# Last sequence of an FFT convolution with spectral mixing: its transformed signal stored by halves of 64 positions, its result tiles in two groups of six

## The chip, the cores and the metric

One core of one Trainium2 chip. The metric is the device time of one execution in microseconds, taken as the median of several runs. Five engines work side by side: TensorE (PE, with its weight loads shown apart as PEld), VectorE (DVE), ScalarE (ACT), GpSimd (POOL) and SyncE (SP), which here issues transfers. Sixteen DMA engines move data between HBM and the on-chip memory (SBUF). TensorE writes its results to PSUM, eight banks of 512 fp32 values on each of 128 partitions.

## The reference

x is 8 sequences of S = 5696 positions with 128 channels, h a filter of the same length. With `n` = 2S:

```
a = irfft(rfft(x, 2S) * rfft(h, 2S))[:, :S]        # long convolution
A = rfft(a);  Y = 0
Y[:, :64] = A[:, :64] mixed by 64 complex 128x128 matrices (w_r, w_i)
u = a + irfft(Y, n=S)
out = u + max(u @ w_ch, 0)                         # float32, 8 x 5696 x 128
```

## The kernel before, in words

A position is written as `J*q + p`, with J = 64, p in 0..63 and q in 0..88 (NQ = 89). The kernel goes over four pairs of sequences (`g_` = 0..3, `b` = 0, 1 within a pair). A first long phase (to about 268 us) makes the spectra, multiplies them by the filter's and leaves them in HBM. The change concerns the second phase, which makes u and the output.

**u tiles.** The 64 values of p are cut into four blocks of 16 (`c_`, NCH = 4), each into two halves of 8. `u_tile` (L787) makes one half: two wide matmuls against `IBs` and 16 narrow ones against `S4a` and `S4b` give 8 p x 89 q in two PSUM banks, and one copy (`evac`, L800) writes those 712 columns as fp16 to the sequence's `UT` buffer. Before, that buffer lies in the natural order of positions: element `J*q + p`. The copies go to ACT or DVE by a fixed pattern of eight (L798: five on ACT, three on DVE).

**Result tiles.** `o_tile` (L841) takes u back as matmul weights: four matmuls of 256 columns (L864) against `WI` (w_ch beside the identity) give u @ w_ch and u, transposed to positions on partitions, in two banks. ACT makes R = relu (L870), DVE adds u (L871) into an output buffer, SP sends the buffer out (L882). With NW = S // 128 = 44, tile r4 takes positions `44*partition + 4*r4 + j`: eleven full tiles (128 partitions x 4 positions), and a twelfth of the last 64 positions with one matmul ("small tile" below). Two neighbouring tiles share one output buffer and one transfer ("wide", 4 KB from each partition). In the last sequence before the change, r4 0 to 7 are wide, 8 to 10 go out singly (2 KB from each partition), and then the small one.

**Order.** All instructions are recorded in program order for each engine; what depends on what is worked out by the recorder. Both kinds of tile take PSUM in turn from four slots of two banks (`LSLOT`), so that the fifth tile waits for the first one's reader. `o_tile` uses seven wide output buffers (`O`), four single ones (`Os`) and three `R` buffers in turn. The order of tiles is the loop at L887 to L903: result tiles stand in a list `todo`, and after each u half some are taken from it. In the last pair (`last`, L894) the order is the four blocks of sequence b = 0 and then the four of b = 1; block number n = 0..7, half 0 and 1:

```
for _ in range((2, 2 + half)[n >= NCH] if last else 1 + half):
```

So two tiles follow each half in n = 0 to 3, and two or three in n = 4 to 7. Each result tile needs all of its sequence's u (L861 names all eight halves). At the last pair's start 24 tiles of the pair before are in `todo`; 12 of b = 0 join after n = 3, and 12 of b = 1 after the loop. I number the last pair's 48 tiles 0 to 47 in the order in which they are taken, and write (n,half) for a u half. Before the change 16 are taken in n = 0 to 3, 20 in n = 4 to 7, and the last twelve (36 to 47) follow when all u is made: the tail. Tiles 11, 23, 35 and 47 are small.

Of the kernel before, what the change touches and what calls it, by code (L numbers as in the profile page):

```python
# [4 lines left out]
P = 128  # L5
# [118 lines left out]
def bass_long_conv_fft__then__afno_spectral_mix_kernel(nc, x, h, moe_w_r, moe_w_i, moe_w_ch, out):  # L124
    B, S, D = x.shape
    M = moe_w_r.shape[0]
    assert D == P and M == 64 and B == 8
    J = 64
    NQ = S // J
# [3 lines left out]
    NP = B // 2  # L133
# [26 lines left out]
    rows = s4.transpose(1, 0, 2, 3).reshape(2 * NK, S)  # L160
# [45 lines left out]
    def at(name, cols, dt, off):  # L206
        return nc.alloc_sbuf_tensor_at(name, [P, cols], dt, offset=off)
# [48 lines left out]
    ZB = 16  # L256
# [13 lines left out]
    u_sb = [at(f"UT{i}", S, F16, u_off[i]) for i in range(4)]  # L270
# [21 lines left out]
    def pv(bank, off, dims, p0=0, n=P):  # L292
        return bass.AP(ps, p0 * 4096 + bank * 512 + off, [[4096, n]] + [list(d) for d in dims])
# [5 lines left out]
    def bank(i):  # L299
        return ("bank", i)  # L300
# [3 lines left out]
    def evac(dst, src, reads, writes, scale=None, eng=None, after=()):  # L304
        e = eng
        if e is None:
            turn[0] ^= 1
            e = "scalar" if turn[0] else "vector"
        if e == "scalar":
            if scale is None:  # L310
                R.add(e, lambda h_: h_.copy(dst, src), reads, writes, after=after)  # L311
            else:
                R.add(e, lambda h_: h_.activation(dst, src, COPY, scale=scale), reads, writes, after=after)  # L313
        elif scale is None:
            R.add(e, lambda h_: h_.tensor_copy(dst, src), reads, writes, after=after)  # L315
        else:
            R.add(e, lambda h_: h_.tensor_scalar_mul(dst, src, scale), reads, writes, after=after)  # L317

    def dma(eng, dst, src, ring, reads=(), writes=(), after=()):
        R.add(eng, lambda h_: h_.dma_start(dst, src), reads, writes, ring=ring, after=after)  # L320

    def mm(o, l, r, st, sp, reads, writes):
        R.add("tensor", lambda h_: h_.matmul(o, l, r, start=st, stop=sp), reads, writes)  # L323
# [3 lines left out]
    def once(key, toks):  # L327
        if key in first:
            return []
        first[key] = 1  # L330
        return list(toks)
# [3 lines left out]
    def turns(name, items):  # L335
        i = ring2.get(name, 0)
        ring2[name] = i + 1
        return items[i % len(items)]
# [101 lines left out]
    for j in range(16):  # L440
        t = turns("h", [0, 2, 4])
# [5 lines left out]
        for i in range(4 if j < 15 else 26):  # L447
# [4 lines left out]
             eng="vector" if j in (3, 7) else "scalar")  # L452
# [264 lines left out]
    for j in range(32):  # L717
        a_tile(j, FOUR)
        if j >= 11 and j % 3 == 2 and (j - 11) // 3 < LH:
            h_ = turns("s", FOUR)  # L720
            filter_tick((j - 11) // 3, [h_, h_ + 1])
    keep(16, turns("s", FOUR))
    for g_ in range(NP):
# [15 lines left out]
        if g_ + 1 < NP:  # L739
            for j in range(6, 32):  # L740
# [3 lines left out]
                if wp and j % 2 == 1:  # L744
                    dst, src_, ring, tok = wp.pop(0)
# [7 lines left out]
        clear_zt(i)  # L753

    LSLOT = [0, 2, 4, 6]
    NCH = J // ZB
    n_ev = [0]
    ahead = {}

    def u_z(i, b, half, alone=False, parts=(0, 1)):  # L760
        g_, c_ = divmod(i, NCH)
        t = ahead.get((i, b, half))
        if t is None:
            t = turns("l", LSLOT)
        z = zt[i % NC]
        for hb in parts:
            if not alone:
                u_c(i, b, half, t, hb, True)
            for pl in range(4):
                for ri in range(2):  # L770
                    pz = half * 8 + hb * 4 + pl
                    so = (c_ * ZB + pz) * NQ
                    n = (P, PB + RB)[ri]
                    mm(pv(t + hb, pl * NQ, [[1, NQ]]), z[ri][0:n, pz * 256 + b * P:pz * 256 + b * P + P], s4_sb[ri][0:n, so:so + NQ],
                       alone and pl == 0 and ri == 0, not alone and pl == 3 and ri == 1, [("zt", i % NC, ri), ("zt0", i % NC), ("s4", ri, 0)] + ([("s4", ri, 1)] if c_ >= NCH // 2 else []), [bank(t + hb)])
        if alone:
            ahead[(i, b, half)] = t
        return t

    def u_c(i, b, half, t, hb, first_):  # L780
        g_, c_ = divmod(i, NCH)
        pl0 = half * 8 + hb * 4
        mm(pv(t + hb, 0, [[1, 4 * NQ]]), c_sb[:, (2 * g_ + b) * P:(2 * g_ + b + 1) * P],
           ib_sb[:, (c_ * ZB + pl0) * NQ:(c_ * ZB + pl0 + 4) * NQ], first_, not first_,
           [("c", g_ // 2), ("ib", 0)] + ([("ib", 1)] if c_ >= NCH // 2 else []), [bank(t + hb)])

    def u_tile(i, b, half):  # L787
        g_, c_ = divmod(i, NCH)
        t = ahead.get((i, b, half))
        if t is None:  # L790
            t = u_z(i, b, half)
        else:
            for hb in range(2):
                u_c(i, b, half, t, hb, False)
        ub = (g_ % 2) * 2 + b
        old = {0: WT, 1: WT, 2: U_ALL, 3: U_ALL}[ub]
        n_ev[0] += 1
        e = "scalar" if n_ev[0] % 8 in (0, 2, 3, 5, 7) else "vector"  # L798
        src = pv(t, 0, [[1, NQ], [512, 2], [NQ, 4]])
        evac(bass.AP(u_sb[ub], c_ * ZB + half * 8, [[S, P], [J, NQ], [4, 2], [1, 4]]),  # L800
             src, [bank(t), bank(t + 1)], [("u_", ub, 2 * c_ + half)], eng=e, after=once(("u", ub), old))

    XTT = [(n, g_) for g_ in range(NP) for n in ("xt", "xtn")]
    reflect("vector", s4_sb[0], P, 0, ("s4", 0), M_ALL[1:4])
# [13 lines left out]
    for hb in range(2):  # L818
        evac(bass.AP(y_sb, hb * 32 * B, [[2 * M * B, P], [B, 32], [M * B, 2], [1, B]]),
             pv(6 + hb, 0, [[2 * B, 32], [B, 2], [1, B]]), [bank(6 + hb)], [("y", hb)], eng="vector" if hb else "scalar",  # L820
             after=ZY)
# [16 lines left out]
    NW = S // P  # L838
    TAIL = S - NW * P

    def o_tile(g_, b, r4):  # L841
        ub = (g_ % 2) * 2 + b
        bb = 2 * g_ + b
        t = turns("l", LSLOT)
        i = n_o[0]
        n_o[0] += 1
        full = r4 < NW // 4
        last_ = (g_, b) == (NP - 1, 1)
        wide = r4 < (8 if last_ else NW // 4 // 2 * 2)
        big = wide or (last_ and full)  # L850
        h_ = r4 % 2 if wide else 0
        if big:
            if not h_:
                o_cur[0] = turns("o8", list(range(NO8)))
            ob, key, old = o8_sb[o_cur[0]], ("o8", o_cur[0]), o8_old[o_cur[0]]
        else:
            k_ = turns("os", list(range(NO)))
            ob, key, old = o_sb[k_], ("os", k_), o_old[k_]
        OW = 1024 if big else 512
        n, rows = (4, P) if full else (1, TAIL)  # L860
        rd = [("u_", ub, c_) for c_ in range(2 * NCH)] + [("wch",), ("i16",)]  # L861
        for j in range(n):
            lh = bass.AP(u_sb[ub], 4 * r4 + j, [[S, P], [NW, P]]) if full else u_sb[ub][:, NW * P:S]
            mm(pv(t + j // 2, (j % 2) * 256, [[1, 256]], 0, rows), lh, WI, True, True, rd, [bank(t + j // 2)])  # L864
        bk = [bank(t), bank(t + 1)] if full else [bank(t)]
        rs = r_sb[i % NR]
        rv = bass.AP(rs, 0, [[512, rows], [P, n], [1, P]])
        ov = bass.AP(ob, h_ * 512, [[OW, rows], [P, n], [1, P]])
        src_r, src_u = pv(t, 0, [[256, n], [1, P]], 0, rows), pv(t, P, [[256, n], [1, P]], 0, rows)
        R.add("scalar", lambda e: e.activation(rv, src_r, RELU), bk, [("r", i % NR)], after=once(("r", i % NR), G_ALL + XTT + [("y", 0), ("y", 1), ("id",)]))  # L870
        R.add("vector", lambda e: e.tensor_tensor(ov, src_u, rv, ADD), bk + [("r", i % NR)],  # L871
              [key + (h_,)], after=once(key, old))
        if wide and not h_:
            return
        w_ = (2 if wide else 1) * 4 * D
        if full:
            dst = bass.AP(out.tensor, out.offset + bb * S * D + (4 * r4 - 4 * h_) * D, [[NW * D, P], [1, w_]])
            src = ob[:, 0:w_]
        else:
            dst = bass.AP(out.tensor, out.offset + bb * S * D + NW * P * D, [[D, TAIL], [1, D]])  # L880
            src = ob[0:TAIL, 0:P]
        dma("sync", dst, src, "o", [key + (v_,) for v_ in range(h_ + 1)])  # L882

    todo = []
    NB = NCH * NP
    NW4 = NW // 4 + 1
    for g_ in range(NP):  # L887
        last = g_ == NP - 1
        order = [(c_, b) for b in range(2) for c_ in range(NCH)] if last else [(c_, b) for c_ in range(NCH) for b in range(2)]
        for n, (c_, b) in enumerate(order):  # L890
            i = NCH * g_ + c_
            for half in range(2):
                u_tile(i, b, half)
                for _ in range((2, 2 + half)[n >= NCH] if last else 1 + half):  # L894
                    if todo:
                        o_tile(*todo.pop(0))
            if b == 1 and i + NC < NB:
                load_zt(i + NC)
            if last and n == NCH - 1:
                todo += [(g_, 0, r4) for r4 in range(NW4)]  # L900
        todo += [(g_, b, r4) for b in range(1 if last else 0, 2) for r4 in range(NW4)]
    while todo:
        o_tile(*todo.pop(0))  # L903
    R.add("sync", lambda e: e.nop(), [], [("o8", i, v_) for i in range(NO8) for v_ in range(2)] + [("os", i, 0) for i in range(NO)])
# [31 lines left out]
```

## Time and profile before

| | |
|---|---|
| median of 3 runs (lowest, highest) | 385.36 us (385.15, 385.92) |
| the profiled execution: its own time | 385.31 us |
| its span in the profile | 383.2 us |
| busy share of the span: PE, DVE, ACT, POOL | 94%, 79%, 81%, 22% |
| mean granted clock of TensorE | 0.992 |
| output transfers on SP (O and Os) | 57 |

The span runs from the first to the last instruction that the profile shows; the execution's own time is 2.1 us longer. Times in the text are counted from the span's start. "Busy" of PE counts matmuls that overlap, so the start of the next tile's first matmul says more than the busy share. Transfers are issued by SP and land later; the profile gives for each group the median time from issue to landing.

### The profile page before, as it was taken

The numbers are of one execution on the slowest core, as the hardware profiler recorded it, in microseconds if no ns is written. First come the engines' busy times: TensorE is split into PE (matmuls) and PEld (weight loads), VectorE is DVE, ScalarE is ACT, GpSimd is POOL, SyncE is SP. The second block draws the span as 40 slices with busy tenths as digits, with TensorE's granted clock in tenths as the row PEclk, the third lists the DMA queues.
The fourth block names the chain that finished last, engine by engine and source line by source line (L and its number), as shares of the span: only waits on it lengthen the run. The fifth ranks groups of instructions, "written<-read, shape, count | busy, mean of one in ns | idle before, by whom it ended". The sixth has DMA issues, their size and how long they took to land.

```text
span 383.2 us, 12465 instructions
## 1 busy us (share of the span) xinstructions
PE 360.0 (94%) x5346; PEld 277.7 (72%) x5346; DVE 303.1 (79%) x346; ACT 310.7 (81%) x489; POOL 84.4 (22%) x134
## 2 busy tenths in 40 slices
PE   7789899999989999989999899999999999999992
PEld 7778766667856667856657766668898988898871
DVE  3549899988998998989998988766347766777784
ACT  8469689998989997899997899994566776777783
POOL 8703011100733210832212312427000000000000
PEclk9999999999999999999999999998999999999998
DMA  7999959988999995999995899999999999999776
GB/s 140 208 286 362 251 141 240 241 230 240 94 126 202 259 262 167 123 123 246 247 256 129 113 329 347 331 382 399 381 394 359 402 407 417 403 403 361 290 281 275
DMA packets 87201, 103.94 MB, mean 271 GB/s; under 512 B 22883, under 2 KB 72675, under 8 KB 83591
## 3 DMA queue, kind: packets, MB, share of 16 engines
q1 hardware_dynamic: 62667, 67.76, 50.9%
q0 software_dynamic: 24480, 35.40, 43.8%
q8 instruction: 42, 0.69, 0.7%
q14 instruction: 12, 0.10, 0.1%
HBM read 70.61 MB, written 51.12 MB: 318 GB/s over the span
## 4 chain that ended last, share of the span: by engine, by line
PE 73%; DVE 7%; DMA 6%; ACT 6%; issue 3%; POOL 3%; DVEq 0%; POOLq 0%
PE ps L323 73%; DMA Xr<-in_x_dram 4%; DVE As L317 2%; DMA Xt<-in_x_dram 2%; DVE U L630 2%; POOL Xr L320 2%; ACT As L313 2%; ACT R L870 1%; ACT Zs L311 1%; ACT UT L311 1%; POOL Hin L320 1%; DVE Xin L365 1%; DVE Hs L315 1%; ACT Zt L311 1%; ACT Xs L311 1%
## 5 line engine op out<-in xcount | busy, mean ns | idle before, releaser
L638 DVE TENSOR_TENSOR U<-Xs,Hs 128x2048 f16<-128x2048 f16 (+1 forms) x73 | 86.9, 1193 | 13.4 <-ACT Xs L311 12.5
L323 PE MATMUL ps<-U,Wc 128*128 128x512 f16 (+1 forms) x368 | 94.1, 376 | 0.5 <-DVE U L630 0.5
L311 ACT CAST Xs<-ps 128x1024 f16<-128x1024 f32 (+1 forms) x77 | 75.2, 980 | 11.9 <-PE ps L323 6.9
L311 ACT CAST Zs<-ps 128x512 f16<-128x512 f32 (+1 forms) x132 | 69.3, 597 | 1.8 <-PE ps L323 1.8
L871 DVE TENSOR_TENSOR O<-ps,R 128x512 f32<-128x512 f32 x81 | 52.5, 686 | 19.8 <-ACT R L870 12.5
L870 ACT ACTIVATE R<-ps 128x512 f32<-128x512 f32 x96 | 50.9, 573 | 14.3 <-PE ps L323 13.9
L317 DVE TENSOR_SCALAR As<-ps 128x720 f16<-128x720 f32 x70 | 57.7, 886 | 5.2 <-PE ps L323 4.6
L323 PE MATMUL ps<-F,Xin 128*128 128x180 f16 x512 | 53.7, 249 | 3.8 <-DVE Xin L365 2.5
L323 PE MATMUL ps<-As,M 64*128 64x128 f16 x1440 | 50.3, 217 | 3.5 <-DVE U L630 2.9
L323 PEld LDWEIGHTS ps<-F,Xin 128*128 128x128 f16 x512 | 44.4, 155 | 12.6 <-DVE As L317 2.8
L323 PE MATMUL ps<-WI,UT 128*128 128x256 f16 x360 | 51.8, 278 | 0.5 <-DVE O L871 0.4
L313 ACT ACTIVATE As<-ps 128x720 f16<-128x720 f32 (+1 forms) x61 | 45.7, 769 | 7.9 <-PE ps L323 6.4
L323 PEld LDWEIGHTS ps<-U,Wc 128*128 128x128 f16 x368 | 28.6, 97 | 29.4 <-ACT Zs L311 3.7
L323 PEld LDWEIGHTS ps<-As,M 64*128 64x128 f16 x1440 | 40.6, 94 | 9.7 <-DVE U L630 3.6
L311 ACT CAST UT<-ps 128x712 f16<-128x712 f32 x40 | 30.0, 752 | 18.0 <-PE ps L323 17.0
L323 PEld LDWEIGHTS ps<-WI,UT 128*128 128x128 f16 x360 | 39.3, 152 | 4.2 <-issue 1.9
L323 PE MATMUL ps<-IBs,C 128*128 128x356 f16 x128 | 39.9, 321 | 0.6
L320 POOL DMA_DIRECT2D Xt<-in_x_dram x40 | 21.4, 540 | 80.3 <-PE ps L323 79.8
L323 PEld LDWEIGHTS ps<-G,Zs 128*128 128x128 f16 x512 | 26.1, 96 | 14.5 <-ACT Zs L311 2.0
L638 DVE TENSOR_TENSOR U<-ps,Hs 128x2048 f16<-128x2048 f32 x15 | 34.3, 2285 | 0.0
L323 PE MATMUL ps<-G,Zs 128*128 128x128 f16 (+2 forms) x512 | 32.3, 192 | 0.1
L311 ACT CAST Zt<-ps 128x512 f16<-128x512 f32 x52 | 28.6, 627 | 0.3 <-PE ps L323 0.3
(88 smaller groups left out, 502.1 us busy)
## 6 DMA issues: line engine op xcount, KB each, us to landing
out_dram<-O SPq DMA_DIRECT2D x39, 512.0 KB, 7.8
zscr<-Zs SPq DMA_DIRECT2D x62, 256.0 KB, 6.8
zscr<-Zt SPq DMA_DIRECT2D x26, 256.0 KB, 6.2
Xt<-in_x_dram POOLq DMA_DIRECT2D x20, 320.0 KB, 7.2
W<-wscr POOLq DMA_DIRECT2D x4, 1024.0 KB, 6.7
M<-cM POOLq DMA_DIRECT2D x5, 720.0 KB, 17.6
ZT0a<-zscr SPq DMA_DIRECT2D x3, 1024.0 KB, 9.0
Hs<-Hs SPq DMA_DIRECT2D x44, 64.0 KB, 6.0
```

The lines of the kernel that those rows point to most:

```text
L311: R.add(e, lambda h_: h_.copy(dst, src), reads, writes, after=after)
L313: R.add(e, lambda h_: h_.activation(dst, src, COPY, scale=scale), reads, writes, after=after)
L315: R.add(e, lambda h_: h_.tensor_copy(dst, src), reads, writes, after=after)
L317: R.add(e, lambda h_: h_.tensor_scalar_mul(dst, src, scale), reads, writes, after=after)
L320: R.add(eng, lambda h_: h_.dma_start(dst, src), reads, writes, ring=ring, after=after)
L323: R.add("tensor", lambda h_: h_.matmul(o, l, r, start=st, stop=sp), reads, writes)
L365: R.add("vector", lambda e: e.tensor_copy(bass.AP(x_sb, i * XN * XS, [[XW, NQ], [XS, XN], [1, D]]), src), list(toks) + XZ, [("xin", i)])
L630: R.add("vector", lambda e, b=b, s_=s_: e.tensor_tensor(bass.AP(u_s[i], b * 512, [[2048, P], [1024, 2], [1, n * D]]), s_, hv, MULT), [tok, ...
L638: R.add("vector", lambda e: e.tensor_tensor(uv, src, hv, MULT), bk + [("h", t, 0), ("h", t, 1, 0), ("h", t, 1, J)], [("u", i)])
L870: R.add("scalar", lambda e: e.activation(rv, src_r, RELU), bk, [("r", i % NR)], after=once(("r", i % NR), G_ALL + XTT + [("y", 0), ("y", 1 ...
L871: R.add("vector", lambda e: e.tensor_tensor(ov, src_u, rv, ADD), bk + [("r", i % NR)], [key + (h_,)], after=once(key, old))
```

## The change

For the last sequence alone (last pair, b = 1):

- the copy of a u half writes to a new order of `UT`: first the half of p (0 to 31, 32 to 63), then p modulo 8, then q, then the eighth within the half. A copy so writes single fp16 values 8 bytes apart, and reads its PSUM columns in their own order;
- its twelve result tiles are numbered by half of p (`hf`), group of q (`qg`, of 32, 32 and 25 q) and `jh`; the weights of one matmul are 128 (or 100) neighbouring columns, which stand for 32 (25) q times 4 eighths. There is no small tile in this sequence: eight tiles have 128 rows and four have 100. A tile waits only for the four u copies of its own half of p;
- tiles of r4 0 to 9 go out in pairs, r4 10 and 11 singly; the destination in HBM is written as `nq` x 4 x 4 KB (or 2 KB);
- six tiles join `todo` after n = 5, the other six after n = 7;
- in the last pair two tiles follow each half 0, three each half 1, in all eight blocks.

In the built programs PE has the same instructions otherwise; DVE and ACT have the same number, and SP one transfer fewer. With the numbering above, the last pair takes five tiles in each block: 40 in the loop, eight (40 to 47) after it. Tiles 36 to 41 are the first half's six and 42 to 47 the second's; the pairs with 100 rows are 40 and 41, and the single 46 and 47.

```
+    QG, QA8 = P // 4, J // 16
...
         src = pv(t, 0, [[1, NQ], [512, 2], [NQ, 4]])
-        evac(bass.AP(u_sb[ub], c_ * ZB + half * 8, [[S, P], [J, NQ], [4, 2], [1, 4]]),
-             src, [bank(t), bank(t + 1)], [("u_", ub, 2 * c_ + half)], eng=e, after=once(("u", ub), old))
+        dst = bass.AP(u_sb[ub], c_ * ZB + half * 8, [[S, P], [J, NQ], [4, 2], [1, 4]])
+        if (g_, b) == (NP - 1, 1):
+            src = pv(t, 0, [[512, 2], [NQ, 4], [1, NQ]])
+            dst = bass.AP(u_sb[ub], c_ // 2 * NQ * (J // 2) + c_ % 2 * 2 + half, [[S, P], [4 * NQ * QA8, 2], [NQ * QA8, 4], [QA8, NQ]])
+        evac(dst, src, [bank(t), bank(t + 1)], [("u_", ub, 2 * c_ + half)], eng=e, after=once(("u", ub), old))
...
-        full = r4 < NW // 4
-        last_ = (g_, b) == (NP - 1, 1)
-        wide = r4 < (8 if last_ else NW // 4 // 2 * 2)
-        big = wide or (last_ and full)
+        if last_:
+            hf, qg, jh = r4 // 6, r4 % 6 // 2, r4 % 2
+            nq = min(QG, NQ - QG * qg)
+            p_at = J * QG * qg + J // 2 * hf + 4 * jh
+        full = last_ or r4 < NW // 4
+        wide = r4 < (10 if last_ else NW // 4 // 2 * 2)
+        big = wide or last_
...
-        n, rows = (4, P) if full else (1, TAIL)
-        rd = [("u_", ub, c_) for c_ in range(2 * NCH)] + [("wch",), ("i16",)]
+        n, rows = (4, nq * QA8 if last_ else P) if full else (1, TAIL)
+        rd = [("u_", ub, c_) for c_ in (range(NCH * hf, NCH * hf + NCH) if last_ else range(2 * NCH))] + [("wch",), ("i16",)]
         for j in range(n):
-            lh = bass.AP(u_sb[ub], 4 * r4 + j, [[S, P], [NW, P]]) if full else u_sb[ub][:, NW * P:S]
+            if last_:
+                o_ = ((8 * hf + 4 * jh + j) * NQ + QG * qg) * QA8
+                lh = u_sb[ub][:, o_:o_ + nq * QA8]
+            else:
+                lh = bass.AP(u_sb[ub], 4 * r4 + j, [[S, P], [NW, P]]) if full else u_sb[ub][:, NW * P:S]
...
-        if full:
+        if last_:
+            dst = bass.AP(out.tensor, out.offset + (bb * S + p_at - 4 * h_) * D, [[J * D, nq], [8 * D, QA8], [1, w_]])
+            src = ob[0:rows, 0:w_]
+        elif full:
...
-                for _ in range((2, 2 + half)[n >= NCH] if last else 1 + half):
+                for _ in range(2 + half if last else 1 + half):
...
             if last and n == NCH - 1:
                 todo += [(g_, 0, r4) for r4 in range(NW4)]
-        todo += [(g_, b, r4) for b in range(1 if last else 0, 2) for r4 in range(NW4)]
+            if last and n in (NCH + 1, 2 * NCH - 1):
+                todo += [(g_, 1, r4) for r4 in (range(6) if n == NCH + 1 else range(6, 12))]
+        if not last:
+            todo += [(g_, b, r4) for b in range(2) for r4 in range(NW4)]
```

## The prediction on record

> **What bounds the kernel now.** I read the page's slices first (PE near 9 tenths until the last two of 40), then the chain of waits that ended last, over the last 54 us, then the timelines of PE, DVE and SP, and last the transfers by window.
>
> The chain from 335 us is nearly all PE until PE waits for a copy. These are rows of it:
>
> ```profile
> 363.60 0.28 ACT R L870
> 363.88 0.82 DVE UT L315
> 364.70 0.05 issue
> 364.75 3.05 PE ps L323 x44
> ```
>
> Three result tiles after a u half fill the other three PSUM slots, so the next half needs the very slot whose copy still stands on DVE behind two additions. The timeline of PE gives the price:
>
> ```profile
> 361.96 0.31 PE L323 MATMUL ps<-IBs,C 128*128 128x356 f16 x1
> ...
> 362.94 1.73 PE L323 MATMUL ps<-WI,UT 128*128 128x256 f16 x12
> 364.75 0.32 PE L323 MATMUL ps<-IBs,C 128*128 128x356 f16 x1
> ...
> 366.64 0.31 PE L323 MATMUL ps<-IBs,C 128*128 128x356 f16 x1
> ```
>
> A u half begins at its first `IBs` matmul: half (6,1) with three tiles takes 2.79 us, (7,0) with two 1.89. Of the starts I use more: 335.37 (0,0), 339.15 (1,0), 343.11 (2,0), 347.06 (3,0), 351.02 (4,0), 352.90 (4,1), 355.37 (5,0), 357.45 (5,1), 360.06 (6,0). I call the last one, 366.64, X.
>
> Then the tail, on DVE and in SP's issues:
>
> ```profile
> 369.18 0.69 DVE L871 TENSOR_TENSOR O<-ps,R 128x512 f32<-128x512 f32 x1 [0.60 <-ACT R L870]
> 369.79 0.87 DVE L871 TENSOR_TENSOR Os<-ps,R 128x512 f32<-128x512 f32 x2
> 370.68 6.80 DVE L871 TENSOR_TENSOR O<-ps,R 128x512 f32<-128x512 f32 x11
> 377.39 0.27 DVE L871 TENSOR_TENSOR Os<-ps,R 64x128 f32<-64x128 f32 x1
> ```
>
> DVE does a full tile each 6.80/11 = 0.618 us without a gap; it is the tail's engine. SP issues the last transfer at 378.50; it lands 4.3 us later and the span ends 0.4 after that: X + 16.56. The transfers in that stretch:
>
> ```profile
> q1 hardware_dynamic: 222, 0.84, 102.5%
> ...
> out_dram<-O SPq DMA_DIRECT2D x3, 256.0 KB, 5.1
> ```
>
> From 376 to 378 us all 16 DMA engines are full. 1.025 x 16 x 2 us for 0.84 MB is 39 us of one engine for each MB (372 to 378 gives 40; I take 39.5). From 362 to 366 us, with queues short, 512 KB lands in 2.6 us; 0.524 x 39.5/16 = 1.29 of it is moving, so 1.3 is fixed.
>
> **The change, part by part.** Sums are made against the profiled execution: 385.31 us, 2.1 beyond its span of 383.2, and 0.05 below the median.
>
> *Four tiles move ahead of X.* Before, 33 result tiles (two small) precede (7,1); after, 37 (three small). PE is the bound there, so they cost PE at least their matmuls: eight take 0.92 us (336.35 to 337.27), so 3 x 0.46 + 0.12 = 1.5 us. But each makes a half of three tiles, and these have a row: n = 0 to 3 give their copies to ACT and DVE in the same pattern as n = 4 to 7 (the second half's copy on ACT, DVE, DVE, ACT). So: n = 0 takes what n = 4 took, 4.35; n = 1 a spilled-over 2.08 and 2.79, 4.87; n = 2 the 4.69 of n = 6, less 0.13 for its small tile, 4.56; n = 3 1.9 + 2.47 = 4.37. Sum 18.15, before 15.65 (335.37 to 351.02): +2.5. In n = 4 to (7,0) the small tiles 23 and 35 stand elsewhere: (4,0) +0.2, (4,1) -0.35, (5,0) -0.15, (5,1) +0.2, (7,0) -0.13; and (4,0), copied by DVE, now follows a half of three tiles, up to +0.4. I take 0 for these together. X moves by **+2.5**; from below 1.5, from above 4 x (2.79 - 1.89) = 3.6.
>
> *The tail on DVE gets shorter.* After X came two full tiles, a small one, eleven full ones and a small one. Now eleven come: 37 to 47. The first addition again starts at X + 2.54 (behind the last u copy and one R on ACT); eleven at 0.618 end at X + 9.3, before X + 11.0: 1.7 earlier. Tiles 42 to 47 need the last u copy (ACT, 367.82 to 368.57, X + 1.9), with five tiles ahead of them as cover, so that wait is hidden.
>
> *The output's end.* Here is what decides. The transfers of q 64 to 88 are written as 25 x 4 rows, from 100 partitions. From the list of transfers by issuer:
>
> ```profile
> ZT4b<-zscr SPq DMA_DIRECT2D x2, 416.0 KB
> ...
> ZT4b<-zscr POOLq DMA_DIRECT2D x1, 416.0 KB, 10.7
> ```
>
> SP's load of 52 rows has no time to landing (GpSimd's has), since it does not leave sixteen completion marks: in the trace all SP transfers of 128 or 64 rows leave 16, each of 52 rows 14. I read 14 as 13 engines and one mark for the rest: 13 is the largest number up to 16 that divides 52. So SP seems to share a transfer out in equal whole rows of its slowest dimension. For 25 x 4 rows that gives **5 engines** (10, if the 100 partitions alone counted); 32 x 4 rows keep 16.
>
> [...]
>
> On five engines, from X: the pair 40, 41 is added by 2.54 + 5 x 0.618 = 5.6 and issued at 5.85; it needs 0.410 MB x 39.5/5 = 3.24. Behind it in the same engines' queues stand 42/43 and 44/45, 1.29 each, then 46 and 47, each 0.205 x 39.5/5 = 1.62 (the last issued at 9.6, long before its turn). 5.85 + 3.24 + 2.58 + 3.24 + 1.3 = 16.2 at landing, 0.4 to the end: **X + 16.6**, against X + 16.56. All that DVE gains is lost: **0.0** against X.
>
> *Copies with 2-byte steps.* Eight copies write single values 8 bytes apart; no row has that. Nearest: `As<-ps` writes runs of 8 bytes, 720 columns in 0.886 (DVE) and 0.769 (ACT); `UT` runs of 16 bytes, 712 in 0.889 and 0.752. No effect of the run; I take 0. Ends: as fast as ACT's plain 512 columns in 0.60 scaled, no gain; twice as long, with the two DVE copies in the chain at (5,1) and (6,1), +1.8.
>
> *Weights side by side.* Loads of strided `UT` columns take 0.152, of plain ones 0.097, but hide under a matmul's 0.115 (0.92/8); ahead of X only four tiles have them: 0, at most -0.1.
>
> *Output buffers in n = 0 to 3.* DMA is full there (1.01 until 340), but PE being the bound, output per us rises by 20/18.15 over 16/15.65, 8%. Landings of up to 12 us leave some 4 us before a wide buffer is written again, at one wide tile each 2 us and seven of them: 0. If that cover went, DVE would wait and PE behind it; it is in the upper end.
>
> Sum: 385.31 + 2.5 + 0.0 = 387.8; **387.7**.
>
> **Rivals.**
>
> 1. *One of the five is held up.* From 371 to 374 us the profile has an instruction load of 16 KB that takes one engine 1.7 us, and wide transfers then land 2.5 us after their usual time. PE's program is as long, so the load comes again in the tail. If it falls on one of the five, the end is 1.7 later: 389.4.
> 2. *Sixteen engines after all* (the change's transfers are as quick as before's): the last is issued at X + 9.6 and ends 4.3 + 0.4 later, X + 14.3, 2.3 us gained. With +2.5 for X, 385.5. With ten engines, tail about X + 15.3: 386.5.
> 3. *Faster:* sixteen engines, and the moved tiles cost PE its matmuls alone, +1.5: 385.31 - 2.3 + 1.5 = 384.5. It decides where X moves by less than 2.3. For it: DVE is idle a quarter of 345 to 370 us. Against it: 2.79 against 1.89 in the same loop, and the 14 marks.
> 4. *Copies twice as long:* 389.5 with five engines.
>
> **How the numbers follow.** The forecast (five engines, none held up, X near +2.5, range 386.5 to 388.5) 0.50; rival 1 0.22; rival 2 with sixteen 0.12, with ten 0.05; rival 3 0.05; rival 4 0.06. Range **385.8 to 389.7**: it leaves out rival 3, much of sixteen engines, and the dear end of rival 4. A measurement of this kernel can tell about 0.2%, 0.77 us, from no change. Faster by more: rival 3 at its best, 0.05. Within: the rest of it and sixteen engines, 0.13. Slower: 0.82.
>
> **What would show it.** First u half to (7,1) 2 to 3 us longer than 31.27, with PE waiting in (1,1) and (2,1) for DVE's copy; last addition near X + 9.3; SP's 25-row transfers without a time to landing on the page; DMA share well under 1 in the last 4 us (5/16 is 0.31) with the end near X + 16.6. Wrong: landings of 25-row transfers with 16 marks, DMA full until the end, a u copy of 712 above 1 us, or X moved by under 1.5.

## The result, and the profile after

The changed kernel takes 399.23 us, the median of six runs (397.72 to 402.63), against 385.25 (384.12 to 387.4, six) for the kernel before on the same chip: 1.0348 times as long, 95% interval 1.0304 to 1.0391. The profiled execution takes 399.02 us, its span is 396.9, TensorE's mean granted clock 0.978.

Ahead of the last pair the instructions are the same, yet the traces differ: the ACT instructions that take from 250 to 275 us in the kernel before take 25.0 us there, 25.4 after the change and from 25.0 to 30.0 in all the traces below, the longest where the granted clock of that stage is lowest (0.93 before, 0.86 after, 0.73 in e3). So traces are compared from (0,0), the start of the last pair, to the end of the span. Before, that is 47.86 us; after, 60.03: **12.2 us more**, of the 13.7 between the two profiled executions. It splits at X, the start of the last u half:

| | (0,0) | (4,0) | X | first addition of the last run of them | end of the last addition | SP's last issue | end |
|---|---|---|---|---|---|---|---|
| before | 335.37 | +15.65 | +31.27 | X + 2.54 | X + 11.02 | X + 11.85 | X + 16.59 |
| after | 336.91 | +17.65 | +37.84 | X + 3.88 | X + 10.55 | X + 12.44 | X + 22.19 |

X is 6.6 us later in the pair (predicted 2.5), and the stretch behind it 5.6 us longer (predicted 0.0).

The end before has a delay of its own in it. In the profile before, an instruction load of 16 KB starts at 373.28 us and takes 1.74 us. From 371 to 374 us it shows as (packets, MB, share of 16 engines)

```profile
q8 instruction: 1, 0.02, 3.6%
```

One of the sixteen engines is late from then on: the transfer issued at 372.12 has fifteen marks by 374.73 and the sixteenth at 377.11, and by its time I put this down to the load. Of the last transfer's marks fifteen stand at X + 14.5 or earlier and the sixteenth at X + 16.2, and the span ends 0.4 after that. None of e3, e5, e6, e8 and v1 to v3 below has so late an engine at its end. If I take the late 1.7 us off, the pair before would be about 46.2 us instead of 47.86; this is an estimate from one trace, and differences of a microsecond or two against the pair before have to be read with it.

For the first part, the chain of waits that ended last (start, length, engine, tile, line) goes through the copies. Rows of it, after:

```profile
367.63 1.78 ACT UT L311
369.41 1.40 ACT R L882 x3
...
370.84 0.37 DVE O L883
371.21 1.69 DVE UT L315
372.90 0.05 issue
372.95 1.17 PE ps L323 x18
...
374.14 1.76 ACT UT L311
```

In one block two u copies stand in series, one on ACT and one on DVE, and each takes 1.7 us or more; the three R between them (1.40) wait for ACT, and DVE for them. The profile's costliest groups (busy us and mean ns of one; idle time before, and what ended it) show the copies' mean raised:

```profile
L311 ACT CAST UT<-ps 128x712 f16<-128x712 f32 x40 | 35.1, 879 | 19.8 <-PE ps L323 19.1
L315 DVE CAST UT<-ps 128x712 f16<-128x712 f32 x24 | 24.0, 999 | 9.5 <-PE ps L323 9.5
```

A mean of 879 ns hides what happened: 35 of ACT's 40 copies still take 0.752, and five 1.76 to 1.78. So read the timelines, not the mean. On PE, after, with its idle time and what ended it in brackets:

```profile
366.44 0.33 PE L323 MATMUL ps<-IBs,C 128*128 128x356 f16 x1 [0.94 <-DVE UT L315]
...
368.34 0.31 PE L323 MATMUL ps<-IBs,C 128*128 128x356 f16 x1
...
370.76 1.23 PE L323 MATMUL ps<-WI,UT 128*128 128x256 f16 x8 [0.63 <-DVE O L883]
372.95 0.32 PE L323 MATMUL ps<-IBs,C 128*128 128x356 f16 x1 [0.95 <-DVE UT L315]
...
374.75 0.31 PE L323 MATMUL ps<-IBs,C 128*128 128x356 f16 x1
```

Half (6,1) lasts from 368.34 to 372.95, 4.61 us; before it was 2.79. PE now stands idle for the DVE copy, which it did not in this stretch before.

For the second part, DVE's tail after X (374.75):

```profile
378.63 6.67 DVE L883 TENSOR_TENSOR O<-ps,R 128x512 f32<-128x512 f32 x11 [1.38 <-ACT R L882]
```

Eleven additions at 0.606 us (predicted 0.618); they end at 385.30. Then nothing but transfers is left for 11.6 us. Busy time by stretch (window, length; PE, PEld, DVE, ACT, POOL with counts; clock, DMA share, GB/s):

```profile
380.00:385.00 5.00, 3.66 (x25) 2.05 (x24) 5.00 (x9) 4.20 (x8) 0.00 (x0) 1.00 0.66 247
385.00:390.00 5.00, 0.00 (x0) 0.00 (x0) 0.30 (x1) 0.00 (x0) 0.00 (x0) 0.60 0.71 254
390.00:397.00 7.00, 0.00 (x0) 0.00 (x0) 0.00 (x0) 0.00 (x0) 0.00 (x0) 0.50 0.18 59
```

And the transfers issued from 379 us on (count, KB each, median us to landing where 16 marks allow one):

```profile
q1 hardware_dynamic: 891, 2.92, 45.3%
...
out_dram<-O SPq DMA_DIRECT2D x4, 512.0 KB, 4.6
...
out_dram<-O SPq DMA_DIRECT2D x1, 400.0 KB
...
out_dram<-O SPq DMA_DIRECT2D x2, 200.0 KB
```

The 25 x 4 transfers (400 and 200 KB) have no time to landing, as foreseen. Each leaves six marks in the trace, that of tiles 40 and 41 one at 383.01 and five from 387.40 to 387.85: I read this as five engines and one mark for the rest. The marks put the landing of tiles 40 and 41, issued at 381.74, at 387.85 (6.1 us; predicted 4.5), and the last, issued at 387.18, at 396.52 (9.3 us).

### The profile page after: what moved, and what is told of

It is laid out like the page before. It is cut to its first block, busy times and chain, and to the rows that moved or that the text cites. A ratio compares the mean times of both kernels' runs of the same rounds, so it can differ in the third digit from the quotient of the medians.

```text
span 396.9 us, 12465 instructions
## 1 busy us (share of the span) xinstructions
PE 363.6 (92%) x5349; PEld 278.7 (70%) x5349; DVE 306.3 (77%) x346; ACT 315.3 (79%) x489; POOL 84.2 (21%) x134
## 4 chain that ended last, share of the span: by engine, by line
PE 70%; DMA 8%; ACT 7%; DVE 6%; POOL 3%; issue 2%; DVEq 0%; POOLq 0%
PE ps L323 70%; DMA Xt<-in_x_dram 4%; DMA Xr<-in_x_dram 4%; ACT UT L311 3%; DVE As L317 2%; ACT R L882 2%; DVE U L630 2%; POOL Xr L320 2%; ACT As L313 2%; POOL Hin L320 1%; ACT Zs L311 1%; DVE O L883 1%; DVE Xin L365 1%; DVE Hs L315 1%; DVE UT L315 1%
## 5 line engine op out<-in xcount | busy, mean ns | idle before, releaser
L883 DVE TENSOR_TENSOR O<-ps,R 128x512 f32<-128x512 f32 (+1 forms) x82 | 53.0, 686 | 20.0 <-ACT R L882 14.4
L882 ACT ACTIVATE R<-ps 128x512 f32<-128x512 f32 (+1 forms) x96 | 51.5, 580 | 14.0 <-PE ps L323 13.9
L323 PE MATMUL ps<-WI,UT 128*128 128x256 f16 (+1 forms) x363 | 52.7, 278 | 3.2 <-DVE O L883 2.5
L311 ACT CAST UT<-ps 128x712 f16<-128x712 f32 x40 | 35.1, 879 | 19.8 <-PE ps L323 19.1
L323 PEld LDWEIGHTS ps<-WI,UT 128*128 128x128 f16 (+1 forms) x363 | 38.4, 146 | 8.8 <-issue 3.7
L323 PEld LDWEIGHTS ps<-G,Zs 128*128 128x128 f16 x512 | 26.1, 96 | 14.5 <-ACT Zs L311 2.0
L315 DVE CAST UT<-ps 128x712 f16<-128x712 f32 x24 | 24.0, 999 | 9.5 <-PE ps L323 9.5
```

## The experiments

Two questions: what makes the copies slow, and what makes the end late. For the copies my theory is the step of the write, single values 8 bytes apart; the rival is that they read PSUM in its own order now. For the end the theory is few engines; the rivals are the three-dimensional destination itself, and a delay that the slow copies pass on. e8 and v2 ask what it is worth to move tiles ahead of X.

In the table, "pair" is from (0,0) to the end of the span in the trace; ratios are to the kernel before, of timed runs.

| kernel | X from (0,0) | last addition ends | end | pair | ratio (95%) |
|---|---|---|---|---|---|
| before | +31.27 | X + 11.02 | X + 16.59 | 47.86 | |
| after | +37.84 | X + 10.55 | X + 22.19 | 60.03 | 1.0348 (1.0304 to 1.0391) |
| e1_runs16 | +33.53 | X + 9.65 | X + 21.00 | 54.53 | 1.0235 (1.0200 to 1.0269) |
| e2_split16_9 | +37.85 | X + 10.55 | X + 15.76 | 53.61 | 1.0186 (1.0125 to 1.0247) |
| e3_runs16_split | +33.52 | X + 9.65 | X + 14.50 | 48.02 | 1.0024 (0.9986 to 1.0063) |
| e4_before_five | +31.29 | X + 11.02 | X + 25.88 | 57.17 | 1.0262 (1.0218 to 1.0306) |
| e5_before_80_48 | +31.27 | X + 11.02 | X + 16.00 | 47.27 | 1.0003 (0.9965 to 1.0042) |
| e6_before_100_28 | +31.27 | X + 11.02 | X + 17.06 | 48.33 | 1.0081 (1.0046 to 1.0116) |
| e7_copy_steps | +35.53 | X + 14.68 | X + 24.73 | 60.26 | one run, no ratio |
| e8_counts_as_before | +31.27 | X + 11.88 | X + 16.75 | 48.02 | 1.0028 (0.9997 to 1.0058) |
| e9_calm_five | +31.27 | X + 11.01 | X + 17.83 | 49.10 | one run, no ratio |
| v1_eighths | +33.52 | X + 9.64 | X + 13.77 | 47.30 | 1.0024 (0.9981 to 1.0067) |
| v2_eighths_counts | +31.27 | X + 11.87 | X + 16.14 | 47.41 | 1.0052 (1.0011 to 1.0093) |
| v3_copies_on_act | +33.23 | X + 9.63 | X + 13.67 | 46.90 | 1.0031 (0.9999 to 1.0063) |

### The changed kernel without its 2-byte steps (e1), without its 25 x 4 transfers (e2), without both (e3)

e1 keeps the order of tiles and the destinations, but lays u so that a copy writes runs of 8 values (16 bytes), and the weights of a matmul are read with the steps that this needs:

```
-            dst = bass.AP(u_sb[ub], c_ // 2 * NQ * (J // 2) + c_ % 2 * 2 + half, [[S, P], [4 * NQ * QA8, 2], [NQ * QA8, 4], [QA8, NQ]])
+            dst = bass.AP(u_sb[ub], c_ // 2 * NQ * (J // 2) + c_ % 2 * 16 + half * 8, [[S, P], [J // 2, NQ], [4, 2], [1, 4]])
...
+                lh = bass.AP(u_sb[ub], (hf * NQ + QG * qg) * (J // 2) + 4 * jh + j, [[S, P], [8, nq * QA8]])
```

> The changed kernel, but the last sequence's u keeps runs of eight values (16 bytes) inside each half of the positions, so copies write as before the change and the weights are strided by 16 bytes. Theory (copies that write single values 8 bytes apart are what lengthened the loop and delayed the tail; the transfers of 25 x 4 rows on five engines are a second, separate cost): u copies back to 0.75 and 0.89 us, the last pair up to half (7,1) about 33.5 us instead of 37.8, the tail still long because of the five engines; about 392 us. Rival (the copies are long because of what else runs there, or are not what delays): copies stay above 1.5 us and the time near 399 us.

e2 sends each 25 x 4 buffer as 16 x 4 and 9 x 4:

```
+            if nq < QG:
+                for q0, q1 in ((0, 16), (16, nq)):
+                    dma("sync", bass.AP(out.tensor, dst.offset + q0 * J * D, [[J * D, q1 - q0], [8 * D, QA8], [1, w_]]),
+                        ob[q0 * QA8:q1 * QA8, 0:w_], "o", [key + (v_,) for v_ in range(h_ + 1)])
+                return
```

> The changed kernel, but each transfer of 25 x 4 rows is two, of 16 x 4 and 9 x 4 rows; copies as changed. Theory (five engines are the tail's cost): every part of the output leaves on 16 or 9 engines, landings in the tail at most 4.5 us, the end near X + 15 instead of X + 22; about 392 us. Rival (the new destination pattern, runs of 16 KB every 32 KB, is slow on any number of engines, or SP's longer issues are the cost): packets stay far above 0.16 us, landings of 6 to 9 us, about 398 us.

e3 does both:

> The changed kernel with both edits: runs of eight values, and 16 x 4 and 9 x 4 rows in place of 25 x 4. Theory (the two causes are separate and add up): what is left is the four moved tiles, +2.0 to +2.5 us for X, and a tail about 2 us shorter; 384 to 386 us. Rival (pattern or issue cost in the tail): 389 us or more.

Measured: in e1 the copies are back to 0.75 on ACT and 0.89 on DVE, and the pair is 5.5 us shorter than in the changed kernel; e1 undoes the order of reading and of writing together; e7 below tells these apart. A row of DVE's timeline in e1:

```profile
368.06 0.89 DVE L315 CAST UT<-ps 128x712 f16<-128x712 f32 x1
```

In e2 the pair is 6.4 us shorter. In e3, from e1, it is 6.5 shorter, and from e2 5.6. So the two costs add and neither hides in the other. With both gone the pair takes 48.02 us, 0.2 more than before, and the time cannot be told from before. In e2 the transfers from 379 us on:

```profile
q1 hardware_dynamic: 951, 2.92, 70.5%
...
out_dram<-O SPq DMA_DIRECT2D x4, 512.0 KB, 3.2
...
out_dram<-O SPq DMA_DIRECT2D x1, 256.0 KB, 3.0
...
out_dram<-O SPq DMA_DIRECT2D x1, 144.0 KB
...
out_dram<-O SPq DMA_DIRECT2D x2, 72.0 KB
```

The 16 x 4 part lands in 3.0 us with the three-dimensional destination left as it is; a plain transfer of 128 rows needs 2.6 where the queues are short (before, 362 to 366 us). The 9 x 4 parts (144 and 72 KB) have no time to landing; nine engines for them is an estimate from the marks of other transfers. So that pattern costs tenths of a microsecond and not the 6. Both rivals for the end fall: the pattern by this row, the slow copies by e1, which keeps 4.4 us more behind X than predicted with quick copies.

In e1 the end was the miss: X + 21.0 where five engines at their rate gave X + 16.6. Its last microseconds (columns as above):

```profile
384.00:386.00 2.00, 0.00 (x0) 0.00 (x0) 0.00 (x0) 0.00 (x0) 0.00 (x0) 0.50 0.31 88
386.00:388.00 2.00, 0.00 (x0) 0.00 (x0) 0.00 (x0) 0.00 (x0) 0.00 (x0) 0.50 0.33 98
```

A share of 0.31 is 5 of 16 engines fully busy, at 88 GB/s: 17.7 for each. Before, with all sixteen full, it was 420 GB/s at a share of 1.02 (376 to 378 us), 25.8 for each. The next row gives 18.6. The five are not idle between packets; some of their packets last longer. Most keep their length: the median for 4 KB is 0.159 us before and in e1. But of the packets of 2 and 4 KB from X + 6 on, 70 of 659 in e1 take over 1.3 times the median, up to 0.85 us, and all the excess together is 15.4 us; before, it is 21 of 907 and 1.5 us. The trace does not say which engine moved a packet; if all the excess fell on the five, it would be 3.1 us for each. By the rate, and if the same five carry all three transfers of 25 x 4 rows, each of the five has 0.23 MB behind the issue of tiles 40 and 41: 9.1 us at the rate I used, 13.0 at 17.7 GB/s, so 3.9 of the 4.4 (an estimate). At the very end one of the five lands 2.2 us after the other four.

### Few engines in the kernel before (e4, e5, e6, e9)

Nothing of the change is in these; the last wide transfers of the kernel before are only cut into two by rows. N is 125 in e4, 80 in e5, 100 in e6:

```
+        if last_ and r4 in (5, 9, 10):
+            for r0, r1 in ((0, N), (N, P)):
+                dma("sync", bass.AP(out.tensor, dst.offset + r0 * NW * D, [[NW * D, r1 - r0], [1, w_]]),
+                    ob[r0:r1, 0:w_], "o", [key + (v_,) for v_ in range(h_ + 1)])
+            return
```

> The kernel before, with three of the last sequence's transfers (the wide one of r4 4 and 5, the single ones of r4 9 and 10) cut into 125 and 3 rows, nothing else changed; 125 rows should run on five engines, and the destination is the old one. Theory (five engines alone, each moving a 4 KB packet in 0.16 us): 25 x 0.16 + 2 x 25 x 0.084 = 8.2 us in the five engines' queues in place of 2.6, span longer by 3.5 to 4; about 389 us. If packets on five engines also slow down to 0.35 us as in the changed kernel's tail: 393 us or more. Rival (five engines cost nothing, the pattern does): 386 us.

> The kernel before with the same three transfers of the last sequence cut into 80 and 48 rows, both multiples of 16. Theory (the number of engines is what costs): packets stay at 0.16 us, three more issues on SP, time within 1 us of the kernel before. [...]

> The kernel before with the same three transfers cut into 100 and 28 rows, which by the divisor rule go to 10 and 14 engines. Theory (fewer engines cost more than their share of bandwidth): between the 80 and 48 rows and the 125 and 3 rows, 387 to 391 us, 11 and 15 completion marks. Rival (only very few engines hurt): as before, 385 to 386 us.

e9 does it earlier, in the sequence before, where the queues are short: tile r4 = 3 as 125 + 3 rows, tile 7 as 80 + 48.

> The kernel before, with two wide transfers of sequence b = 0 of the last pair cut, in the stretch where queues are short: r4 2 and 3 into 125 and 3 rows, r4 6 and 7 into 80 and 48. Read are their landings and the length of packets. Theory A (five engines move packets at the usual 0.16 us when nothing else crowds): the 125 rows land 25 x 0.16 + 1.3 = 5.3 us after issue. Theory B (a transfer on few engines is slow by itself, its packets 0.2 to 0.6 us): 6.5 us or more. The 80 and 48 rows land in 2.6 to 3.5 us by both.

Measured in e4: 9.3 us more, far above what five engines at the usual rate would give (3.5 to 4), and what was expected if their packets slow down (393 us or more; 395.5). The destination is the old two-dimensional one and all additions end where they did, so neither the pattern nor the work ahead does this. Busy time and transfers (issued from 374 us on) in e4:

```profile
376.00:378.00 2.00, 0.67 (x5) 0.31 (x3) 2.00 (x5) 1.23 (x3) 0.00 (x0) 1.00 0.63 188
...
384.00:386.00 2.00, 0.00 (x0) 0.00 (x0) 0.00 (x0) 0.00 (x0) 0.00 (x0) 0.50 0.30 74
```

```profile
q1 hardware_dynamic: 1034, 2.75, 44.5%
...
out_dram<-O SPq DMA_DIRECT2D x1, 500.0 KB
...
out_dram<-O SPq DMA_DIRECT2D x1, 256.0 KB, 11.4
```

From 384 to 386 us the share of 0.30 is 4.8 of the 16 engines, at 74 GB/s 15.4 for each. A plain transfer of 128 rows (256 KB) issued behind the 125 rows lands after 11.4 us: eleven of its sixteen marks stand within 6.2 us of its issue, the last five later. SP itself is held: three of its issues take 3.13, 1.50 and 2.60 us, where 0.33 is usual; in the tail before the longest is 0.95, in e5 1.46.

e5 has the same number of extra transfers, both parts on sixteen engines (16 marks each), and the timed runs show no cost (1.0003). So the cut and the number of transfers are not what makes e4 slow. The cut lengthens packets in a small way all the same: from X + 6 on 109 of 916 packets of 2 and 4 KB take over 1.3 times the median, up to 0.59 us, with an excess of 13.5 us in all (e4: 161 of 914, 30.5 us). Spread over sixteen engines that is 0.8 us for each, and the pair, 47.27, is longer than the 46.2 estimated for the kernel before without its late engine. Transfers issued from 378 us in e5, and from 374 in e6:

```profile
out_dram<-O SPq DMA_DIRECT2D x1, 320.0 KB, 3.2
...
out_dram<-O SPq DMA_DIRECT2D x1, 192.0 KB, 3.8
```

```profile
out_dram<-O SPq DMA_DIRECT2D x1, 400.0 KB
...
out_dram<-O SPq DMA_DIRECT2D x1, 112.0 KB
```

In e6 the parts leave 11 and 15 marks, which I read as ten and fourteen engines. The pair takes 0.5 us more than before, 2.1 more than the estimated 46.2, and the timed runs are 0.81% slower (0.46 to 1.16%), about 3 us. So the theory named for e6 holds: a cost between those of e5 and e4, whose size the trace alone would understate. In e9, over the stretch around the 125 rows:

```profile
360.00:364.00 4.00, 3.92 (x53) 3.40 (x54) 2.85 (x6) 2.89 (x5) 0.00 (x0) 1.00 0.84 328
364.00:368.00 4.00, 3.92 (x50) 3.29 (x50) 3.19 (x6) 3.22 (x6) 0.00 (x0) 1.00 0.29 77
368.00:372.00 4.00, 3.58 (x33) 2.83 (x30) 3.36 (x7) 3.48 (x8) 0.00 (x0) 1.00 0.86 270
```

The 125 rows, issued at 364.45 with nothing much in the queues, land after 6.75 us where the rate I used would give 5.3, and 77 GB/s at a share of 0.29 is 16.6 for each busy engine. So the low rate belongs to transfers on five engines also away from a crowd. PE, DVE and ACT go on as before beside it (3.92 us of 4 for PE), and X and the last addition stay where they were. But the delay is not all covered: the transfers behind land later (the 80 and 48 rows after 5.0 and 4.8 us, where 2.6 to 3.5 was expected), SP's last issue comes at X + 13.4 instead of X + 11.85, and the end is 1.2 us later than before.

### Steps of the copy (e7)

In the changed kernel the four blocks of the last sequence's u write with steps of their own, in other places of the buffer; the last block keeps steps of 8 bytes but writes q first and p within it, so that no two neighbours in time share 16 bytes, and it reads PSUM in the old order:

```
+            st_, at_ = ((1, half * 8 * NQ), (2, 16 * NQ + half), (4, 32 * NQ + half), (4, 32 * NQ + 2 + half))[c_]
+            if c_ < 3:
+                src = pv(t, 0, [[512, 2], [NQ, 4], [1, NQ]])
+                dst = bass.AP(u_sb[ub], at_, [[S, P], [4 * NQ * st_, 2], [NQ * st_, 4], [st_, NQ]])
+            else:
+                dst = bass.AP(u_sb[ub], at_, [[S, P], [st_, NQ], [4 * NQ * st_, 2], [NQ * st_, 4]])
```

> The changed kernel with another step in each block's copy of the last sequence: block 0 writes 712 values side by side (2 bytes apart), block 1 values 4 bytes apart, block 2 8 bytes apart, block 3 8 bytes apart but in the order q first, p inside, as the copies before read PSUM. The last sequence's u stands in the wrong places, so its output is not the reference's. Read are the copies' durations on ACT and DVE. Theory A (what counts is how many values fall into 16 bytes, at least four needed): 0.75 and 0.89 us for steps of 2 and 4 bytes, 1.75 for 8. Theory B (any single value is a write of its own): 1.75 for 4 bytes too, 0.75 for 2. Theory C (the order in which PSUM is read): block 3 back at 0.75.

ACT's copies of the four blocks, from its timeline in e7, in the order of blocks:

```profile
357.13 0.75 ACT L311 CAST UT<-ps 128x712 f16<-128x712 f32 x1 [0.50 <-PE ps L323]
...
359.60 0.98 ACT L311 CAST UT<-ps 128x712 f16<-128x712 f32 x1 [0.39 <-PE ps L323]
...
364.57 1.78 ACT L311 CAST UT<-ps 128x712 f16<-128x712 f32 x1 [0.72 <-PE ps L323]
...
371.08 3.39 ACT L311 CAST UT<-ps 128x712 f16<-128x712 f32 x1 [1.51 <-PE ps L323]
```

DVE's, of the first three blocks:

```profile
355.72 0.89 DVE L315 CAST UT<-ps 128x712 f16<-128x712 f32 x1
...
362.35 0.97 DVE L315 CAST UT<-ps 128x712 f16<-128x712 f32 x1
...
368.07 1.76 DVE L315 CAST UT<-ps 128x712 f16<-128x712 f32 x1
```

On ACT, eight values in each 16 bytes cost 0.75, four 0.98, two 1.78, one 3.39. The first block reads PSUM in the changed kernel's order and is quick, the last reads it in the old order and is slowest: the order of reading is innocent, and the write decides. 712 columns touch 178 stretches of 16 bytes with four values in each, 356 with two, 712 with one: 0.98/178, 1.78/356 and 3.39/712 are 5.5, 5.0 and 4.8 ns for each, and from one of the three to the next the copy grows by 4.5 ns for each stretch more. Counted by 8 bytes the same rows would give 2.8, 2.5 and 4.8 ns, by 32 bytes 11.0, 10.0 and 4.8: of the three sizes 16 is the one that gives all three rows nearly one price.

The number of stretches is not all of it, though. The `As<-ps` copies of the first phase touch 180 stretches, in each of them four values that stand side by side in 8 bytes (the runs are 256 bytes apart), and ACT does their 720 columns in 0.781 us before (58 copies, with a scale). Four values 4 bytes apart cost 0.98. So four neighbours cost next to nothing more, and the price holds for values that stand apart.

### What the moved tiles are worth (e8), and two better layouts (v1, v2, v3)

e8 is e3 with the old numbers of tiles behind each half:

```
-                for _ in range(2 + half if last else 1 + half):
+                for _ in range((2, 2 + half)[n >= NCH] if last else 1 + half):
```

> The changed kernel with runs of eight values and 16 x 4 and 9 x 4 rows, and with two result tiles after each half in the first four blocks as before the change, so that twelve tiles follow the last u half again. Theory (moving four tiles costs X 2.0 us and shortens the tail by about 1.9): within 0.7 us of the same kernel with the tiles moved, 386 us; X back at 31.3 us after the last pair's start. Rival (moving them is a real gain that something else hid): 1.5 us or more slower, 387.5 us.

X is 2.25 us later in e3 than in e8, and the stretch behind it 2.25 shorter: the pair takes 48.02 in both. Four tiles cost ahead of X just what they save behind it, also with the output on sixteen and nine engines.

v1 sets the tiles by even and odd eighths of p: the four half-0 copies first and then the four half-1, runs of 16 bytes, and rows of the destination evenly spaced, so that all transfers but a rest of 4 rows should use sixteen engines (an estimate from the sixteen marks of 128, 80 and 48 rows). v2 is v1 with the old numbers of tiles:

```
+            dst = bass.AP(u_sb[ub], half * (S // 2) + c_ * 8, [[S, P], [J // 2, NQ], [4, 2], [1, 4]])
...
+            p_at = J * QG * qg + 8 * hf + 4 * jh
```

> A version meant to keep the change's idea without its two costs: the last sequence's u goes by even and odd eighths of the 64 positions (all first halves of the four blocks, then all second halves), so that result tiles are plain rows 16 positions apart; copies write runs of eight values; the groups with 100 rows go out as 96 and 4 rows, and the two single tiles at the end have 128. Five tiles in each block, eight in the tail. Theory (moved tiles cost X 2.0, the tail ends 3 us earlier after X when its transfers run on 16 engines and without third dimensions): 384 to 385 us, 0.1 to 0.4% faster than before. Rival (the tail's end is set by the landing of the last transfers, whatever comes before): 386 us.

> The same, with two result tiles after each half in the first four blocks as before the change, twelve tiles in the tail. Theory: X back, tail as before, 385 to 386 us, 0.5 to 1 us slower than with the tiles moved. Rival (moving tiles is no gain): equal or faster than with the tiles moved.

v3 is v1 with more of the last pair's copies on ACT:

```
+        if g_ == NP - 1:
+            e = "vector" if n_ev[0] % 8 == 6 else "scalar"
```

> The version by eighths with five tiles a block, and in the last pair seven of eight u copies on ACT, so that a half of three tiles seldom waits for a copy that stands behind additions on DVE. Theory (the 2.8 us of such halves is DVE's copy, those copied by ACT take 2.35 to 2.5): X 1 us earlier, the end of the last pair 47.3 us after its start becomes 46.5; the time 384 to 386 us, the difference too small for the times but seen in the trace. Rival (ACT becomes the bound with two copies and five relu a block): X no earlier, or later.

In the traces the pair is 0.56 us (v1), 0.45 (v2) and 0.96 (v3) shorter than before, but longer than the 46.2 estimated without the late engine. The timed runs show no gain: v1 1.0024 and v3 1.0031, with intervals that reach down to 0.9981 and 0.9999, and v2's lies above 1. So none of them is shown to beat the kernel before. v1 missed its 384 to 385 us (386.9), and v2 is 0.1 us longer in the pair than v1 instead of 0.5 to 1: moving the tiles is no gain here either. In v3 X comes 0.3 us earlier than in v1, where 1 us was expected, and the pair takes 46.90 instead of 46.5.

## Why the prediction was wrong, point by point

It said slower, by 2.4 us; it was slower by 14. Both large terms that it set to zero were not.

- **The step that failed first: "No effect of the run; I take 0".** The runs of 8 and 16 bytes in the rows at hand cost the same, and I read on from there to single values. (The prediction's 0.886 and 0.769 for `As<-ps` are means with a few copies of 360 columns in them; those of 720 columns alone take 0.901 and 0.781.) They were rows from the flat end: runs of four and of eight neighbours lose nothing, single values with two in each 16 bytes take about twice as long (1.78 us on ACT and 1.76 on DVE, against 0.75 and 0.89). Measured: 5.5 us (e1, e2 against e3). Rival 4 had the right duration, "twice as long", but its price, +1.8, was three times too low. It counted the two DVE copies of (5,1) and (6,1). In truth an ACT copy (+1.03) and a DVE copy (+0.87) stand in series in each of these halves, through the R between them: the changed kernel loses 1.71 and 1.82 us against e3 in the two, 0.77 in (4,1), and 4.3 with the rest. The tail gets the remaining 1.2: the last u copy and the first R behind it move the first addition from X + 2.54 to X + 3.88.
- **The second: the output's end, "All that DVE gains is lost: 0.0".** Five engines was right: six marks for 25 x 4 rows. The size was not: 39.5 us of one engine for each MB, taken where sixteen are full, does not hold on five: in e1 they move 17.7 to 18.6 GB/s each instead of 25.8, since about a tenth of the packets take longer. In e1, with quick copies, the end is at X + 21.0 and not X + 16.6: 4.4 us more. Against sixteen and nine engines (e2) the few cost 6.4 us, where I had counted on 2.3. The X + 16.56 that this was set against held the late engine's 1.7 us, which the prediction left in the base and named in rival 1 alone. Rival 1, "one of the five is held up", names something seen (2.2 us at the end), but not its cause: the profile has the instruction load of 16 KB at 378.36 us, long before; what holds the fifth engine stays open.
- **The number of engines: held.** In each case here the marks are as many as the largest number up to 16 that divides the rows (of 25 x 4, the 25), and one more where that number is below 16: six for 25 x 4 rows (five engines), 11 for 100, 15 for 28, 16 for 80 and for 48. The sum to X + 16.6 also sets all transfers of 25 x 4 rows on the same five engines. No run shows this, since the trace does not say which engine moved a packet; what it shows after the change is that of the sixteen marks of each of the two transfers of 32 x 4 rows behind tiles 40 and 41, issued at 382.94 and 384.13, eleven stand by 387.41 and 388.65, and five come late, from 388.64 to 389.11 and from 389.88 to 392.02.
- **X later by 2.5 for the moved tiles: right.** 2.25 (e3 against e8). In the first four blocks it is 2.0, +17.65 against +15.65: 4.24, 4.69, 4.27 and 4.45 us where the prediction had 4.35, 4.87, 4.56 and 4.37.
- **DVE's end at X + 9.3: right** without the slow copies, 9.65 in e1. An addition takes 0.606 us in the changed kernel (predicted 0.618) and 0.647 in e1, where DVE waits between some of them.
- **Output buffers: 0, held**; the blocks n = 0 to 3 are no longer than the copies' pattern makes them. Weights side by side were not tried apart from the layout of u; no wait in the trace names them.
- Rival 2's arithmetic, +2.5 and -2.3 with sixteen engines, comes near what e3 does, +2.25 and -2.09, but the second number by luck: the last transfer is issued at X + 11.7 and not X + 9.6, and lands after 2.4 us and not 4.3, which held the late engine.
- About 1.5 us of the difference between the two profiled executions lies ahead of the last pair, where the instructions are the same; none of the runs gives a reason to put it down to the change.

Two of the signs named in advance showed the errors: a u copy above 1 us, and the end far from X + 16.6. The range failed since both zero terms missed on the same side. That of the copies had bounds from the path of one engine, and for the rate on few engines I had no bound at all, though no row showed it.

## What to carry to other kernels

When a copy's destination is laid out anew, count how many values fall into each 16 bytes of the write, and whether they stand side by side: four apart make the copy 0.1 to 0.2 us longer here (0.97 instead of 0.89 us on DVE, 0.98 instead of 0.75 on ACT), two take twice as long (1.76 and 1.78), and what it costs is read along the chain, over every engine that takes such copies. When an output is cut into new shapes, look for a number of rows that divides by 16, or cut it into parts that do: 128, 80 and 48 rows left sixteen marks here, 100 rows eleven, and on five engines the same bytes cost 6 to 9 us at the end of this kernel (6.4 in the changed kernel against e2, 9.3 in e4), and in two transfers on sixteen nothing that the timed runs show (e5). A row of the profile that shows no effect between two sizes says nothing of a third beyond them.

## What the runs showed of the hardware that was not expected

- In e7 a copy whose values stand apart took about 5 ns for each 16-byte stretch touched anew (4.8 to 5.5 on ACT), where this exceeds the 0.75 us on ACT or 0.89 us on DVE that 712 columns take side by side. Both engines show it alike: 1.78 and 1.76 us at two values in each. Four neighbours in each did not pay it (0.781 us for 180 stretches on ACT, before).
- With transfers on five engines three things were slower: their own packets (15.4 in e4 to 18.6 GB/s in e1 for each busy engine, against 25.8), later transfers on sixteen (11.4 us to landing in e4, 6.3 instead of 2.6 in e9), and SP's own issues (1.62, 1.34 and 1.14 us in the changed kernel, up to 3.13 in e4, usually 0.33). It does not go in proportion: with 100 and 28 rows (11 and 15 marks) the timed runs are 0.81% slower (e6), with 125 and 3 rows (a share of 0.30, 4.8 engines) 2.62% (e4).
- One of sixteen engines stayed late for the rest of the kernel from the time of an instruction load of 16 KB on (373.28 us, 1.74 long): before, 2.4 us just after it, and still 1.7 at the end. In e6 a lateness of 2.3 us at the same place is made up by the end.
- Why some packets take several times their usual length (0.85 us for 4 KB instead of 0.159) stays open. They come on five engines and, spread over more, also where transfers on sixteen are cut by rows (e5).
